# One ScalarE function table, scores of two heads from 64-row products, and a weight decode without Abs, in a fused attention and softplus expert kernel

## The chip, the cores and the metric

The kernel runs on one core of one Trainium2 chip. The core has a matrix engine (TensorE, PE in the profile, with its weight loads as PEld), a vector engine (VectorE, DVE), an engine for functions of one element (ScalarE, ACT), a general engine (GpSimd, POOL) and a queue engine (SyncE, SP) that issues transfers. The metric is the time of one execution on the device in microseconds, the median of the runs.

## The reference, cut to what matters

Attention over 4 batches, 8 heads, 576 tokens and 64 dimensions with a causal mask, mixed with a linear memory term by a gate per head, and then a two-layer expert with softplus between the layers (2304 tokens, 512 to 2048 to 512). Inputs q, k, v, M_prev, z_prev, beta are float32; the two expert weights come as float64.

```python
scores = scale * (q @ k^T)                    # scale = 1/8, causal mask
a = exp(scores - rowmax(scores))
a /= a.sum(-1) + 1e-9
local = a @ v
phi(x) = where(x > 0, x, exp(x) - 1) + 1
mem_out = (phi(q) @ M_prev) / (phi(q) @ z_prev + 1e-6)
g = 1 / (1 + exp(-beta))
x = g * mem_out + (1 - g) * local             # tokens x 512
h = x @ w_in
y = (max(h, 0) + log1p(exp(-abs(h)))) @ w_out # softplus between the layers
```

## The kernel before, in words

**Attention.** The work is cut into 16 units, one for each batch and pair of heads; a unit has five chunks of queries (four of 128 rows and one of 64). `emit_S` (lines 296 to 324) makes one chunk: scores of both heads into a PSUM tile `s`, a causal mask added by a product with an identity, the negated row maximum `nm` on VectorE, and the exponential on ScalarE straight from PSUM (line 318, or 322 for the last chunk), which also sums the row into `l`. The queries that feed the scores are copies `qs`, scaled by 1/8, in which the other head's 64 rows are zero, so that each head's product takes all 128 rows (line 301 with `qs`; `q1`, lines 239 to 243, makes the copies on ScalarE). `emit_split` (326 to 364) turns the exponentials into float16 high and low parts: high on GpSimd (line 342), low on VectorE (line 344), then a transposing transfer on the SP queue. `emit_pv` (line 385) multiplies by the values, 64 columns of the array for each head, the heads taking turns. The preparation of the next unit (`prep_items`: `v0` scale of the values, `f1` and `f2` phi(q), `f3` the memory product, `v1` and `v2` the float16 values) is spread over the chunks of the present one.

**Expert.** `emit_h` (line 144) makes one block of h: 12 products (`mm3`, line 134) of 288 tokens, with float32 numbers carried as two float32r parts. `emit_g` applies softplus to it as max(h,0) + log1p(exp(-|h|)) in eight instructions on ScalarE, GpSimd and VectorE (lines 159 to 166 and the helper at line 83), and splits the result into two parts (lines 89 and 83). A second group of 12 products takes it to the output accumulators `acc`. There are 16 blocks of d_ff in three groups of 5, 5 and 6. For the first group, four of the eight token blocks (20 calls of `emit_g`) are woven into the attention as filler, against a credit that grows with each chunk; the other 108 calls come after it. The weights arrive as the bits of float64 and are decoded by `split64` (lines 114 to 128): 32 pieces of 128x512, 10 during the attention, 22 after it while the products of the group before run.

**Order.** Each engine runs its own queue in order. A scheduler that works with modelled durations and with the priorities given in the code fixes the order of each queue when the program is built. Every ScalarE function comes from one table, loaded once at line 423.

## Time and profile before

| | before |
|---|---|
| time, median of 3 runs | 722.13 us (721.14 to 722.64) |
| span of the profiled execution | 718.0 us |
| PE / PEld busy | 636.2 us (89%) / 560.7 us (78%) |
| DVE busy | 585.8 us (82%) |
| ACT busy | 480.1 us (67%) |
| POOL busy | 389.4 us (54%) |
| chain that ended last, by engine | PE 40%, DVE 38%, ACT 7%, issue 6%, DMA 5%, POOL 4% |

The span runs from the first to the last instruction; the profile gives no other time for that execution, and the 4.1 us between the span and the median lie around it. The engines overlap, so that their busy times add up to far more than the span. PE's busy time holds the latency of its products too: a PE that is 100% busy in a stretch need not be at its fastest. The chain follows the work back from the last instruction, at each step to what released it.

### The profile page before, as it was taken

Reading aid. Unit: us, or ns where it says so; the run is one execution under the profiler, and the core shown is the slowest. Engines: PE = TensorE matmul, PEld = TensorE weight load, DVE = VectorE, ACT = ScalarE, POOL = GpSimd, SP = SyncE. Lnnn points to the kernel's source line nnn. Section 1 sums busy time; section 2 is a strip of 40 time slices with the busy share of each in tenths; the row PEclk is TensorE's granted clock in tenths of the full one; section 3 lists DMA queues with packets and bytes.
Section 4 is the critical chain, followed back from the end, with each engine's and each line's share of the span. In section 5 each row is a group of like instructions: output and inputs, shape, how many; then the busy total and the mean of one; then the engine's idle time right before and its main releaser. Section 6 shows DMA issues by size and latency. Waiting matters only on the chain.

```text
span 718.0 us, 13325 instructions
## 1 busy us (share of the span) xinstructions
PE 636.2 (89%) x4488; PEld 560.7 (78%) x4488; DVE 585.8 (82%) x1271; ACT 480.1 (67%) x1314; POOL 389.4 (54%) x495
## 2 busy tenths in 40 slices
PE   6587768979899889989788897888999999999997
PEld 5455546757777657768777896778999999999997
DVE  5899999996988998995899989998777655655644
ACT  7576677767767866864777685666666666666653
POOL 3456647774865864762466665565444334344342
PEclk9698978799999999999999999999999999999999
DMA  4988787576688678637522211210000000000101
GB/s 146 170 175 192 175 175 166 122 120 142 116 149 177 125 126 195 113 53 170 195 89 89 89 59 63 85 60 1 1 1 1 1 34 34 34 17 35 34 20 64
DMA packets 124179, 68.51 MB, mean 95 GB/s; under 512 B 105680, under 2 KB 113872, under 8 KB 124112
## 3 DMA queue, kind: packets, MB, share of 16 engines
q1 hardware_dynamic: 124112, 67.67, 40.9%
q8 instruction: 35, 0.57, 0.3%
q14 instruction: 32, 0.26, 0.1%
HBM read 34.89 MB, written 7.08 MB: 58 GB/s over the span
## 4 chain that ended last, share of the span: by engine, by line
PE 40%; DVE 38%; ACT 7%; issue 6%; DMA 5%; POOL 4%; SPq 0%; POOLq 0%; ACTq 0%; DVEq 0%
PE acc L134 16%; PE hp L134 16%; DVE PHL L344 6%; DVE l L166 4%; DVE c L165 3%; PE s L301 3%; DVE xhl L83 3%; DVE nm L316 3%; DVE wu L123 3%; DVE g L83 2%; DVE wu L125 2%; POOL PHL L342 2%; DVE wu L120 2%; ACT P L318 2%; DMA mq<-in_nat_dram 2%
## 5 line engine op out<-in xcount | busy, mean ns | idle before, releaser
L134 PE MATMUL hp<-xhl,w 128*128 128x288 f32 x1536 | 237.5, 303 | 8.6 <-ACT r L161 7.4
L134 PEld LDWEIGHTS hp<-xhl,w 128*128 128x128 f32 x1536 | 216.5, 193 | 12.3 <-ACT r L161 8.6
L134 PE MATMUL acc<-g,w 128*128 128x288 f32 x1296 | 190.0, 297 | 19.1 <-DVE g L83 9.4
L134 PEld LDWEIGHTS acc<-g,w 128*128 128x128 f32 x1296 | 176.7, 188 | 24.0 <-DVE g L83 11.8
L83 POOL TENSOR_TENSOR l<-l,c 128x288 f32<-128x288 f32 x128 | 116.0, 907 | 117.0 <-DVE l L166 109.2
L342 POOL TENSOR_SCALAR PHL<-P,rr 128x128 f16<-128x128 f32 (+3 forms) x128 | 85.4, 680 | 70.0 <-DVE rr L338 15.0
L163 POOL TENSOR_SCALAR c<-e 128x288 f32<-128x288 f32 x128 | 66.2, 518 | 85.1 <-ACT e L162 83.3
L301 PE MATMUL s<-kp,qs 128*128 128x128 f32 (+3 forms) x256 | 93.5, 494 | 9.8 <-ACT P L318 8.4
L344 DVE SCALAR_TENSOR_TENSOR PHL<-P,rr,PHL 128x128 f16<-128x128 f32 (+3 forms) x128 | 93.8, 751 | 7.3 <-POOL PHL L342 7.0
L165 DVE SCALAR_TENSOR_TENSOR c<-c,e 128x288 f32<-128x288 f32 x128 | 66.0, 516 | 37.4 <-ACT l L164 36.5
L318 ACT ACTIVATE P<-s,nm 128x128 f32<-128x128 f32 (+3 forms) x128 | 66.3, 525 | 41.6 <-DVE nm L316 36.6
L159 ACT ACTIVATE e<-hp 128x288 f32<-128x288 f32 x128 | 52.6, 411 | 57.1 <-PE hp L134 38.0
L164 ACT ACTIVATE l<-c 128x288 f32<-128x288 f32 x128 | 56.9, 445 | 45.8 <-DVE g L83 29.2
L83 DVE TENSOR_TENSOR g<-l,g 128x288 fp32r<-128x288 f32 x108 | 65.0, 603 | 26.5 <-ACT g L89 25.5
L89 ACT CAST g<-l 128x288 fp32r<-128x288 f32 x128 | 55.2, 432 | 28.0 <-POOL l L83 27.2
L166 DVE TENSOR_TENSOR l<-r,l 128x288 f32<-128x288 f32 x128 | 70.1, 548 | 0.0
L301 PEld LDWEIGHTS s<-kp,qs 128*128 128x128 f32 x256 | 46.7, 215 | 28.3 <-ACT P L318 10.6
L162 ACT ACTIVATE e<-e 128x288 f32<-128x288 f32 x128 | 57.3, 449 | 0.0
L83 POOL TENSOR_TENSOR w<-wu,w 128x512 fp32r<-128x512 f32 x32 | 49.1, 1535 | 14.2 <-ACT w L89 14.1
L385 PEld LDWEIGHTS <-vb 128*64 128x64 f16 x640 | 35.1, 116 | 26.4 <-issue 12.3
L316 DVE TENSOR_REDUCE nm<-s 128x2 f32<-128x256 f32 (+1 forms) x64 | 51.7, 810 | 4.7 <-PE s L304 4.6
L161 ACT ACTIVATE r<-hp 128x288 f32<-128x288 f32 x128 | 52.5, 410 | 3.5 <-DVE l L166 3.5
(85 smaller groups left out, 914.6 us busy)
## 6 DMA issues: line engine op xcount, KB each, us to landing
ws<-in_w_in_dram SPq DMA_DIRECT2D x16, 512.0 KB, 3.4
ws<-in_w_out_dram SPq DMA_DIRECT2D x16, 512.0 KB, 3.4
mq<-in_nat_dram SPq DMA_DIRECT2D x16, 353.0 KB, 3.4
va<-in_nat_dram SPq DMA_DIRECT2D x16, 320.0 KB, 3.2
kp<-in_nat_dram SPq DMA_DIRECT2D x16, 288.0 KB, 3.6
out_dram<-ps SPq DMA_DIRECT2D x32, 144.0 KB, 1.8
part<-pb SPq DMA_DIRECT2D x16, 144.0 KB, 2.4
ps<-part SPq DMA_DIRECT2D x4, 576.0 KB, 8.8
```

The lines of the kernel that those rows point to most:

```text
L83: eng.tensor_tensor(out=out, in0=in0, in1=in1, op=ALU.subtract)
L134: nc.tensor.matmul(out, lhsT=l, rhs=r, start=start and i == 0, stop=stop and i == n - 1)
L162: A.activation(out=e, in_=e, func=AF.Exp, scale=-1.0)
L163: P.tensor_scalar(out=c, in0=e, scalar1=1.0, scalar2=1.0, op0=ALU.mult, op1=ALU.add)
L164: A.activation(out=l, in_=c, func=AF.Ln)
L165: V.scalar_tensor_tensor(out=c, in0=c, scalar=-1.0, in1=e, op0=ALU.add, op1=ALU.subtract)
L166: V.tensor_tensor(out=l, in0=h, in1=l, op=ALU.add)
L301: nc.tensor.matmul(s[:, h, :n], lhsT=u.qs[:, 512 * h + c * 128:512 * h + (c + 1) * 128], rhs=u.kp[:, :n], start=True, stop=True)
L316: V.tensor_reduce(out=nm, in_=s[:, :, :n], op=ALU.max, axis=AX.X, negate=True)
L318: A.activation(out=pt[:, h * n:h * n + n], in_=s[:, h, :n], func=AF.Exp, bias=nm[:, h:h + 1], accum_out=l[:, h:h + 1])
L342: P.tensor_scalar(out=o[:, :, 0, h, :], in0=src, scalar1=r[:, h:h + 1], scalar2=0.0, op0=ALU.mult, op1=ALU.add)
L344: V.scalar_tensor_tensor(out=o[:, :, 1, h, :], in0=src, scalar=r[:, h:h + 1], in1=o[:, :, 0, h, :], op0=ALU.mult, op1=ALU.subtract)
```

## The change

Softplus replaces Exp and Ln as the one function of the ScalarE table. In `emit_g` one Softplus from PSUM takes the place of seven instructions. In the attention exp(y) is taken as softplus(y - 20), which is exp(y)·e^-20 to within float32 for y at or below 0; the factor e^-20 cancels through the row sums, the gates and the small constants. The scale 1/8 moves into the exponential's own scale, so the row maximum is multiplied by 1/8 and shifted by -20 in an added ScalarE instruction on a 128x2 tile (line 307 of the changed code), between the maximum and the exponential. The copies `qs` go, and each head's scores are a product over its own 64 rows of the query tile; the last chunk takes four products of 64 rows and 64 columns where it took two of 128 and 128. In `split64` the magnitude comes from a shift of the integer bits on VectorE, then a minimum and maximum on GpSimd, where it was ScalarE's Abs and a maximum on VectorE. In `v0` the mean magnitude comes from two Relu passes (of the value and its negative) and two small products, where it was one Abs pass and one product. The gates of beta are computed with Softplus as well.

```diff
 def split64(s, tu, hi, lo):
-        A.activation(out=tu, in_=sw[:, :, 1], func=AF.Abs)
-        V.tensor_scalar(out=tu, in0=tu, scalar1=TINY, scalar2=None, op0=ALU.max)
+        V.tensor_scalar(out=ti, in0=si[:, :, 1], scalar1=1, scalar2=1, op0=ALU.logical_shift_left,
+                        op1=ALU.logical_shift_right)
+        P.tensor_scalar(out=tu, in0=tu, scalar1=3.0e38, scalar2=TINY, op0=ALU.min, op1=ALU.max)
         V.tensor_scalar(out=ti, in0=ti, scalar1=3, scalar2=0x3FFFFFFF, op0=ALU.logical_shift_left,
                         op1=ALU.bitwise_and)
...
 def emit_g(pool, hp, n, cap, gb):
-        e = pool.tile([128, cap], F32, tag="e", name="e", bufs=2)
-        c = pool.tile([128, cap], F32, tag="c", name="c", bufs=2)
-        l = pool.tile([128, cap], F32, tag="l", name="l", bufs=2)
+        l = pool.tile([128, cap], F32, tag="l", name="l", bufs=3)[:, :n]
         g = pool.tile([128, 2, cap], F32R, tag="g", name="g", bufs=gb)
-        e, c, l = e[:, :n], c[:, :n], l[:, :n]
-        A.activation(out=e, in_=hp[:, :n], func=AF.Abs)
-        h = pool.tile([128, cap], F32, tag="r", name="r", bufs=2)[:, :n]
-        A.activation(out=h, in_=hp[:, :n], func=AF.Relu)
-        A.activation(out=e, in_=e, func=AF.Exp, scale=-1.0)
-        P.tensor_scalar(out=c, in0=e, scalar1=1.0, scalar2=1.0, op0=ALU.mult, op1=ALU.add)
-        A.activation(out=l, in_=c, func=AF.Ln)
-        V.scalar_tensor_tensor(out=c, in0=c, scalar=-1.0, in1=e, op0=ALU.add, op1=ALU.subtract)
-        V.tensor_tensor(out=l, in0=h, in1=l, op=ALU.add)
-        sub(P, l, l, c)
+        A.activation(out=l, in_=hp[:, :n], func=AF.Softplus)
         cast(A, g[:, 0, :n], l)
         sub(V if hcnt else P, g[:, 1, :n], l, g[:, 0, :n])
...
 def prep_items(i):
-        def q1():
-            for h in range(2):
-                r = slice(64 * h, 64 * h + 64)
-                A.mul(u.qs[r, 512 * h:512 * h + 512], u.qp[r, 0:512], 0.125)
-                A.mul(u.qs[r, 1024 + 64 * h:1088 + 64 * h], u.qp[r, 512:576], 0.125)
...
-            A.activation(out=jk, in_=u.vst, func=AF.Abs, accum_out=u.sc[:, 3:4])
+            for j, sg in enumerate((1.0, -1.0)):
+                A.activation(out=jk, in_=u.vst, func=AF.Relu, scale=sg, accum_out=u.sc[:, 3 + j:4 + j])
             sp = ps_r.tile([128, 512], F32, tag="sm", name="sp", bufs=1)
-            nc.tensor.matmul(sp[:, 0:1], lhsT=mean, rhs=u.sc[:, 3:4], start=True, stop=True)
+            for j in range(2):
+                nc.tensor.matmul(sp[:, 0:1], lhsT=mean, rhs=u.sc[:, 3 + j:4 + j], start=j == 0, stop=j == 1)
...
-            A.activation(out=u.pe, in_=u.pe, func=AF.Exp, scale=-1.0)
+            A.activation(out=u.pe, in_=u.pe, func=AF.Softplus, scale=-1.0, bias=msh)
...
 def emit_S(u, c):
             for h in range(2):
-                nc.tensor.matmul(s[:, h, :n], lhsT=u.qs[:, 512 * h + c * 128:512 * h + (c + 1) * 128],
-                                 rhs=u.kp[:, :n], start=True, stop=True)
+                r = slice(64 * h, 64 * h + 64)
+                nc.tensor.matmul(s[:, h, :n], lhsT=u.qp[r, c * 128:(c + 1) * 128], rhs=u.kp[r, :n],
+                                 start=True, stop=True)
...
             for i in range(2):
-                nc.tensor.matmul(s[:, i, :288], lhsT=u.qs[:, 1024:1152], rhs=u.kp[:, 288 * i:288 * i + 288],
-                                 start=True, stop=True)
+                for h in range(2):
+                    r = slice(64 * h, 64 * h + 64)
+                    nc.tensor.matmul(s[r, i, :288], lhsT=u.qp[r, 512:576], rhs=u.kp[r, 288 * i:288 * i + 288],
+                                     start=True, stop=True)
...
             V.tensor_reduce(out=nm, in_=s[:, :, :n], op=ALU.max, axis=AX.X, negate=True)
+            A.activation(out=nm, in_=nm, func=AF.Copy, scale=SCALE, bias=-SH)
             for h in range(2):
-                A.activation(out=pt[:, h * n:h * n + n], in_=s[:, h, :n], func=AF.Exp,
-                             bias=nm[:, h:h + 1], accum_out=l[:, h:h + 1])
+                A.activation(out=pt[:, h * n:h * n + n], in_=s[:, h, :n], func=AF.Softplus,
+                             scale=SCALE, bias=nm[:, h:h + 1], accum_out=l[:, h:h + 1])
...
-        A.preload_act_table_set("natural_log_exp_and_others")
+        A.preload_act_table_set("softplus")
```

Left out of the diff: the constants (SH = 20, ESH = e^-20, the tile `msh` that holds -20), the same edit of the exponential in the last chunk, the factor ESH at the small constants of `f2`, `f3` and `emit_split`, and the gates of beta in `consts`.

## Rows read from the trace of the kernel before

**Rows 1.** Busy time of each engine in five stretches. Columns: stretch, its length, busy us (instructions) of PE, PEld, DVE, ACT and POOL, the granted TensorE clock as a share of full speed, the DMA engines' busy share, GB/s.
```profile
0.00:160.00 160.00, 122.82 (x745) 88.20 (x746) 143.67 (x354) 109.37 (x294) 97.24 (x118) 0.85 0.75 161
160.00:328.00 168.00, 154.10 (x1118) 120.70 (x1117) 151.24 (x363) 118.84 (x340) 107.59 (x139) 0.98 0.69 135
328.00:345.00 17.00, 16.27 (x132) 15.09 (x131) 8.58 (x20) 8.95 (x24) 2.55 (x4) 1.00 0.73 193
345.00:500.00 155.00, 128.71 (x887) 122.85 (x886) 148.08 (x244) 107.79 (x286) 94.27 (x101) 0.97 0.23 77
500.00:718.00 218.00, 214.28 (x1615) 213.82 (x1613) 134.26 (x295) 135.11 (x373) 87.77 (x134) 1.00 0.07 23
```

**Rows 2.** The same view in short stretches: one of the attention, one of the last stage.
```profile
259.00:262.50 3.50, 3.50 (x9) 1.39 (x9) 3.22 (x9) 3.07 (x9) 2.83 (x5) 0.64 0.97 152
...
520.00:540.00 20.00, 20.00 (x153) 20.00 (x152) 14.97 (x31) 13.93 (x40) 8.71 (x13) 1.00 0.00 1
```

**Rows 3.** The waits of the stretch 328 to 500 us that hold PE. Columns: engine, its instruction and line, what it waited for, total us, times, longest us.
```profile
PEld acc L134 <- DVE g L83: 11.8, 10, 2.2
PEld hp L134 <- ACT r L161: 8.6, 5, 4.0
PEld acc L134 <- DVE ps L572: 8.0, 7, 1.8
```

**Rows 4.** Instructions of `emit_g`, grouped by line and shape. Columns: line, engine, operation, tiles written and read, shapes, count, busy us in total and mean ns of one, idle time of the engine before them with what ended it.
```profile
L159 ACT ACTIVATE e<-hp 128x288 f32<-128x288 f32 x128 | 52.6, 411 | 57.1 <-PE hp L134 38.0 <-DVE c L165 16.0 <-PE acc L134 2.3
L161 ACT ACTIVATE r<-hp 128x288 f32<-128x288 f32 x128 | 52.5, 410 | 3.5 <-DVE l L166 3.5
L162 ACT ACTIVATE e<-e 128x288 f32<-128x288 f32 x128 | 57.3, 449 | 0.0
L163 POOL TENSOR_SCALAR c<-e 128x288 f32<-128x288 f32 x128 | 66.2, 518 | 85.1 <-ACT e L162 83.3
L164 ACT ACTIVATE l<-c 128x288 f32<-128x288 f32 x128 | 56.9, 445 | 45.8 <-DVE g L83 29.2 <-POOL c L163 16.0
L165 DVE SCALAR_TENSOR_TENSOR c<-c,e 128x288 f32<-128x288 f32 x128 | 66.0, 516 | 37.4 <-ACT l L164 36.5
L166 DVE TENSOR_TENSOR l<-r,l 128x288 f32<-128x288 f32 x128 | 70.1, 548 | 0.0
L83 POOL TENSOR_TENSOR l<-l,c 128x288 f32<-128x288 f32 x128 | 116.0, 907 | 117.0 <-DVE l L166 109.2 <-DVE sc L255 3.9 <-DVE a L278 1.9
L83 DVE TENSOR_TENSOR g<-l,g 128x288 fp32r<-128x288 f32 x108 | 65.0, 603 | 26.5 <-ACT g L89 25.5
```

**Rows 5.** Instructions of `split64`, and the nearest GpSimd instruction of 512 elements with one tensor input; same columns.
```profile
L119 ACT ACTIVATE wu<-ws 128x512 f32<-128x512 f32 x32 | 21.6, 674 | 7.8 <-DMA ws<-in_w_out_dram 4.0 <-DMA ws<-in_w_in_dram 3.1 <-POOL w L83 0.8
L120 DVE TENSOR_SCALAR wu<-wu 128x512 f32<-128x512 f32 x32 | 19.3, 603 | 2.3 <-ACT wu L119 2.0
L121 DVE TENSOR_SCALAR wu<-wu 128x512 int32<-128x512 int32 x32 | 21.1, 659 | 0.3
L123 DVE SCALAR_TENSOR_TENSOR wu<-ws,wu 128x512 int32<-128x512 int32 x32 | 25.7, 803 | 0.2
L342 POOL TENSOR_SCALAR PHL<-P,rr 128x512 f16<-128x512 f32 x32 | 26.6, 843 | 18.1 <-issue 5.2 <-DVE rr L338 4.2 <-DVE a L280 2.8
```

**Rows 6.** The timeline from 348 us, in order of time. Columns: start us, length us, engine, line, operation, tiles, shapes, count, idle before.
```profile
348.57 3.13 POOL L83 TENSOR_TENSOR w<-wu,w 128x512 fp32r<-128x512 f32 x2
...
349.06 1.51 DVE L165 SCALAR_TENSOR_TENSOR c<-c,e 128x288 f32<-128x288 f32 x1
...
351.93 0.45 DVE L165 SCALAR_TENSOR_TENSOR c<-c,e 128x288 f32<-128x288 f32 x1
```

**Rows 7.** ScalarE instructions of the attention's preparation, and the smallest ScalarE instruction of the kernel, with the columns of rows 4.
```profile
L242 ACT ACTIVATE qs<-mq 64x512 f32<-64x512 f32 x32 | 20.0, 626 | 10.1 <-DMA mq<-in_nat_dram 9.8
L250 ACT ACTIVATE vb<-va 128x640 bf16<-128x640 f32 x16 | 11.7, 734 | 1.1 <-PE xp L385 1.0
L410 ACT ACTIVATE bsb<-bsb 128x8 f32<-128x8 f32 x1 | 0.2, 208 | 1.8 <-DMA bsb<-in_beta_dram 1.8
```

**Rows 8.** The longest wait for the row maximum in the stretch 165 to 328 us, with the columns of rows 3.
```profile
ACT P L318 <- DVE nm L316: 20.8, 12, 4.3
```

**Rows 9.** PE's timeline at three score chunks at the full clock (of 128, 512 and 288 columns; four matmul records each, two heads by two passes), at one of 512 columns in the stretch whose clock rows 2 give, and at one group of `emit_pv`; columns of rows 6.
```profile
268.09 0.61 PE L301 MATMUL s<-kp,qs 128*128 128x128 f32 x4
...
219.55 1.94 PE L301 MATMUL s<-kp,qs 128*128 128x512 f32 x4
...
264.17 1.24 PE L308 MATMUL s<-kp,qs 128*128 128x288 f32 x4
...
259.38 3.26 PE L301 MATMUL s<-kp,qs 128*128 128x512 f32 x4
...
222.53 1.72 PE L385 MATMUL xp<-PTB,vb 128*64 128x320 f16 x28
```

**Rows 10.** The forms of the records in that group of `emit_pv` (tile PTB), all units together; columns of rows 4.
```profile
L385 PE MATMUL xp<-PTB,vb 128*64 128x320 f16 x288 | 28.4, 313 | 6.0 <-DMA PTB<-PHL 6.0
L385 PE MATMUL xp<-PTB,vb 128*64 128x192 f16 x96 | 9.7, 252 | 0.0
L385 PE MATMUL xp<-PTB,vb 128*64 128x64 f16 x64 | 5.5, 197 | 0.0
```

**Rows 11.** The load of ScalarE's function table; columns of rows 4.
```profile
L423 ACT ACT_TABLE_LOAD x1 | 1.3, 1283 | 0.7 <-PEq L620 0.7
```

More of the change, by code (lines that the diff above doesn't have):

```diff
@@ L1 @@
+import math
 from collections import deque
@@ L24 @@
 TINY = 2.0 ** -15
+SH = 20.0
+SCALE = 0.125
+ESH = math.exp(-SH)
 GRPS = [5, 5, 6]
@@ L63, in attn_softplus_moe @@
     ident = res.tile([128, 128], F32, name="ident")
+    msh = res.tile([128, 1], F32, name="msh")
     g15 = res.tile([128, H], F32, name="g15")
@@ L219, in attn_softplus_moe @@
     at = attn_ctx.enter_context(tc.tile_pool(name="attn", bufs=1, side="right"))
-    qs_t = [at.tile([128, 1152], F32, name=f"qs{i}") for i in range(2)]
     def loads(i):
         u = units[i]
-        u.qs = qs_t[i % 2]
         b, p = u.b, u.p
@@ L237, in prep_items @@
         p = u.p
-        def q1():
-            for h in range(2):
-                r = slice(64 * h, 64 * h + 64)
-                A.mul(u.qs[r, 512 * h:512 * h + 512], u.qp[r, 0:512], 0.125)
-                A.mul(u.qs[r, 1024 + 64 * h:1088 + 64 * h], u.qp[r, 512:576], 0.125)
         def v0():
-            u.sc = at.tile([128, 4], F32, tag="sc", name="sc", bufs=3)
+            u.sc = at.tile([128, 5], F32, tag="sc", name="sc", bufs=3)
             si = u.sc.bitcast(I32)
@@ L262, in f1 @@
             A.activation(out=u.pe, in_=u.qp, func=AF.Relu, scale=-1.0)
-            A.activation(out=u.pe, in_=u.pe, func=AF.Exp, scale=-1.0)
+            A.activation(out=u.pe, in_=u.pe, func=AF.Softplus, scale=-1.0, bias=msh)
         def f2():
             u.ph = at.tile([128, S], F32, tag="ph", name="ph", bufs=1)
-            A.activation(out=u.ph, in_=u.qp, func=AF.Relu)
+            A.activation(out=u.ph, in_=u.qp, func=AF.Relu, scale=ESH)
             P.tensor_tensor(out=u.ph, in0=u.ph, in1=u.pe, op=ALU.add)
@@ L277, in f3 @@
                 nc.tensor.matmul(t[:, c - c0, :], lhsT=u.ph[:, q0:q0 + 128], rhs=u.mz, start=True, stop=True)
-            V.tensor_scalar(out=a, in0=t[:, :, 128:130], scalar1=1e-6, scalar2=None, op0=ALU.add)
+            V.tensor_scalar(out=a, in0=t[:, :, 128:130], scalar1=1e-6 * ESH, scalar2=None, op0=ALU.add)
             V.reciprocal(out=a, in_=a)
@@ L336, in emit_split @@
             nk = c + 1
-            V.scalar_tensor_tensor(out=r, in0=l, scalar=1e-9, in1=cinv[:, 2 * p:2 * p + 2], op0=ALU.add, op1=ALU.mult)
+            V.scalar_tensor_tensor(out=r, in0=l, scalar=1e-9 * ESH, in1=cinv[:, 2 * p:2 * p + 2], op0=ALU.add, op1=ALU.mult)
             V.reciprocal(out=r, in_=r)
@@ L349, in emit_split @@
             r = r[:, 0:1]
-            V.scalar_tensor_tensor(out=r, in0=l[:, 0:1], scalar=1e-9, in1=cinv4[:, p:p + 1], op0=ALU.add, op1=ALU.mult)
+            V.scalar_tensor_tensor(out=r, in0=l[:, 0:1], scalar=1e-9 * ESH, in1=cinv4[:, p:p + 1], op0=ALU.add, op1=ALU.mult)
             V.reciprocal(out=r, in_=r)
@@ L407, in consts @@
         P.memset(mean, 2.0 ** -7)
-        for t in qs_t:
-            P.memset(t, 0.0)
-        A.activation(out=bsb, in_=bsb, func=AF.Exp, scale=-1.0)
-        V.tensor_scalar(out=bsb, in0=bsb, scalar1=1.0, scalar2=None, op0=ALU.add)
-        V.reciprocal(out=bsb, in_=bsb)
-        V.tensor_scalar(out=cinv, in0=bsb, scalar1=-1.0, scalar2=1.0, op0=ALU.mult, op1=ALU.add)
-        V.tensor_scalar(out=cinv, in0=cinv, scalar1=PSC, scalar2=1e-30, op0=ALU.mult, op1=ALU.max)
+        P.memset(msh, -SH)
+        A.activation(out=cinv, in_=bsb, func=AF.Softplus)
+        A.activation(out=bsb, in_=bsb, func=AF.Softplus, scale=-1.0)
+        A.activation(out=bsb, in_=bsb, func=AF.Softplus, scale=-1.0, bias=msh)
+        A.activation(out=cinv, in_=cinv, func=AF.Softplus, scale=-1.0, bias=msh)
+        V.tensor_scalar(out=cinv, in0=cinv, scalar1=PSC / ESH, scalar2=1e-30, op0=ALU.mult, op1=ALU.max)
         V.reciprocal(out=cinv, in_=cinv)
```

9 lines of the change are left out of this document (5 added, 4 removed).

## The prediction

> **What bounds the kernel now.** I read the busy time by stretches first, because a share over the whole span mixes stages with different limits [rows 1]. Up to 328 us the kernel is in the attention: VectorE is busy 143.7 of the first 160 us (90%) and 151.2 of the next 168 (90%), with PE at 77% and 92%, ScalarE near 70%. From 328 to 345 us PE is full. From 345 to 500 us VectorE is busy 148.1 of 155 us (96%) while PE, at a granted clock of 0.97, is busy 128.7. From 500 us PE is never idle until the tail and VectorE has 62%.
>
> How far PE is from its pace in the third stretch is seen by counting. In the last stage 153 products take 20 us, 130.7 ns each [rows 2]. The 887 products of 345 to 500 us would take 887 x 0.1307 = 115.9 us at that pace; 39.1 us are lost there. The waits of that stage tell to whom: PE's weight loads wait for VectorE's low part of g (11.8 us), for ScalarE's Relu that frees the h tile (8.6), and for VectorE's accumulation (8.0) [rows 3]. So VectorE bounds two stages, PE the rest.
>
> **The change, part by part.**
>
> *emit_g.* Four ScalarE instructions (411, 410, 449, 445 ns) become one that reads the same PSUM tile; the table is not in the trace, so I bound it by the cheapest and dearest of these, 410 to 449, and take 411, that of the one with the same operands: 1.30 us less. VectorE loses 516 + 548 = 1.06 us, GpSimd 518 + 907 = 1.43 us [rows 4]. What remains, cast and subtraction, is unchanged. For 20 calls in the attention that is 21.3 us of VectorE; in 345 to 500 us, with 887/24 = 37 calls, 39.3 us; the rest lie where PE is full, and give nothing.
>
> *split64.* ScalarE loses 0.67 us for each piece. VectorE swaps a maximum (0.60) for a shift whose input has a stride of two; between the row of the same operation (0.66) and the one that reads the strided tile with a second input (0.80) I take 0.66, so +0.06, at most +0.20, and below nothing only as far as less GpSimd work lies beside it. GpSimd gains an instruction of one input; its row is 0.84 [rows 5]. VectorE's next instruction waits for it, and queued behind on VectorE are low parts of g and PE's accumulation. If the scheduler finds other VectorE work to put between, this costs nothing; if never, 22 x 0.84 = 18.5 us in the expert stage. I take 7, a third, and call this an estimate: the like wait today, for Abs, ends in 2.0 us in all [rows 5], but ScalarE's queue is freer than GpSimd's.
>
> *Attention, ScalarE.* The 512-column part of `q1` goes, 20.0 us; the second pass in `v0` adds 16 x 0.73 = 11.7; 80 instructions on `nm` add 80 x 0.21 = 16.6 by the smallest row [rows 7]; emit_g gives back 20 x 1.30 = 26.1, the ten decodes 6.7. Net 24 us less of 228 [rows 1], on an engine that is no bound. The instruction on `nm` matters by its place: it stands between maximum and exponential, where ScalarE already waits 20.8 us in the second stretch [rows 8], and it holds the score tile 0.2 us longer. With VectorE at 90% other units' work covers it; where the start has no cover, some 15 chunks at 0.2, it costs 3 us, and 80 x 0.21 = 17 us if it is covered nowhere.
>
> *Scores.* A chunk is four matmul records, two passes for each head: 0.61 us at 128 columns, 1.94 at 512 [rows 9]; between these lie 256 and 384 at some 1.05 and 1.50, so 5.1 us a unit, and 1.24 for the last chunk. Two products on different halves of the array can run beside each other: `emit_pv` shows it for columns. Its 28 records in 1.72 us [rows 9] are 18 of 320, 6 of 192 and 4 of 64 columns [rows 10], 7168 columns; at 130.7 ns for 288 [rows 2] they would take 3.25 us one by one. But there the heads alternate. Here each head brings two passes in a row, so that in order only the second of one head meets the first of the other: three slots of four, -1.3 us; the last chunk has eight records where it had four and fits them in five, +0.3. Net -1.0 a unit, 16 us of PE in the attention. The ends: all pairs meet, -2.55 x 16 = -41; none does, and the last chunk doubles, +20. The second small product in `v0` is two records of one column, less than half of the 0.61 us of four records of 128, so under 5 us of PE in all, inside these ends.
>
> *Loads.* The query tile is now read until the unit's last scores, as the key tile is already, so the load into its buffer starts later; on the SP queue the keys, the values and the transposing transfers stand behind it, but the keys waited for the same scores before. ScalarE waits 9.8 us for this load today, at `q1` [rows 7]; `f1` takes its place, and may wait as long again. 0 to +10 us; I take 0, since ScalarE has slack and VectorE needs what comes of it only a chunk later.
>
> The Trainium skill (TensorEngine Tiling (Array Packing), Key Properties) says against this that a change of tiling mode drains TensorE; each chunk would change it twice, around the mask product. No row isolates a drain; by that rule the 16 us would be less, and since VectorE sets the pace of both stretches the sum would hardly move.
>
> *The sum by stages, on the span of 718.0.* First 160 us: 5 of the 20 calls, 5.3 us of VectorE, less the 3 us of `nm`: -3 (bounds +3, when none of half the 80 links is covered, and -12, when the start without `qs` and less GpSimd traffic also count). 160 to 328: 15 calls, 16.0 us of VectorE; PE, busy 154.1 of 168, must follow, and may with half of the 16 us from the scores: 146. I take -15 (bounds: 0, if the stretches where PE is full only grow or `f1` waits; -30 if all pairs meet). 328 to 345: nothing. 345 to 500: VectorE's work falls to 148.1 - 39.3 + 1 = 110, under PE's 115.9, so PE becomes the bound; 39.1 less the 7 for the decode: -32 (bounds -20 and -39). Last stage: nothing, PE is the bound and its products are untouched. In all -50: a span of 668, and with the 4.1 us between span and median of the runs **672 us**.
>
> **Rivals.**
>
> *A. The attention gives nothing* (0 in both stretches, or the two cancel): the added link on `nm` and the decode's detour keep VectorE idle where it now works. For it: 80 added links, 20.8 us of waits at that place already. Against: 21 us of VectorE work leave a stage that is 90% VectorE. Time 722 - 32 = 690.
>
> *B. GpSimd's new instruction holds VectorE.* Today a VectorE instruction with two inputs takes 1.51 us while GpSimd subtracts and 0.45 beside an idle GpSimd [rows 6]. If each of the 22 new instructions stops VectorE for its own 0.84 us and the waits on it are exposed as well, the expert stage keeps 18.5 us of its loss: -20 there, 722 - 38 = 684. Against: GpSimd loses 37 x 1.43 = 53 us in that stage and gains 18.5, so VectorE should be held less, not more. The Trainium skill (GPSIMD Engine Reference, Specifications) has GpSimd sharing its SBUF interface with VectorE's instructions of two SBUF inputs; by that rule, the trace agrees.
>
> *C. More than forecast:* score pairs meet fully, and both stretches of the attention reach their lower bounds: -42 there, -32 to -39 later: 641 to 648. Against: VectorE's other 274 us of both stretches stay.
>
> *D. Slower: the clock.* The change takes work from PE in the attention, where its clock is already granted at only 0.85 on the mean over the first stretch with PE 77% busy [rows 1]. If PE has more pauses and the clock of the second stretch drops to the lower of its levels (1.2 GHz), its work lengthens: the four records of 512 columns took 3.26 us at a clock of 0.64 and 1.94 at full [rows 2, 9], a factor of 1.68, so 154 us become 259: +91 in that stretch against -35 elsewhere, some 778. It decides from about 47% of that stretch on (91 against the 15 not gained there, and 35). Against: the filler products keep that stretch at 0.98, and they run closer together afterwards.
>
> *E. The change doesn't do what it says:* if one of the functions used is not in the new table, it is loaded again and again, at 1.28 us each [rows 11]; 39 reloads undo the whole gain, and every emit_g would bring two. Against: only Softplus, Relu and Copy remain, and one table served four functions so far.
>
> **How the numbers follow.** Forecast (660 to 682): 0.50. A (683 to 698): 0.18; B (680 to 690): 0.12; C (640 to 659): 0.12; D: 0.04; E: 0.02; 0.02 for an attention that eats up what the expert stage gains. The range 650 to 697 holds the forecast, A, B and half of C, 0.86, less a few hundredths for the queue order, which the scheduler makes anew. A measurement of this kernel can tell 0.2% from no change. Faster by more than that: 0.93 (forecast, A, B, C and half of the last case); within it 0.02; slower 0.05 (nearly all of D and E).
>
> **What would show it.** In the profile of after: an expert stage where PE is never idle from some 310 us on, with 153 products in each 20 us while decodes still run; VectorE under 85% busy there; VectorE's busy time lower by 128 x 1.06 = 136 us and GpSimd's by 182 - 27 = 155. The last score accumulation ends near 310 us, not 328. Score chunks of 512 columns take some 1.5 us (three slots), not 1.94 nor 1.0. One load of the table. I am wrong if the expert stage still shows VectorE at 95% (then the decode's detour counts), if the attention ends at 325 us or later (A), or if the granted clock of the second stretch is under 0.9 (D).

## The result, and the profile after

The changed kernel takes **696.96 us** (median of 4 runs, 696.07 to 698.73) where the kernel before took 721.63 beside it: a ratio of 0.9676, interval 0.9649 to 0.9703. The forecast was 672. The time lies at the very end of the stated range, and of the 50 us forecast 25 came. The profiled execution has a span of 695.3 us. One version below, e3, ran in two groups, six runs of ten at 713 to 720 us and four at 701 to 708, and its ratio is of the faster four.

Busy time of each engine by stretches, after, in the columns of rows 1 and with the same limits:

```profile
0.00:160.00 160.00, 126.63 (x749) 80.17 (x750) 128.94 (x313) 90.27 (x263) 82.94 (x111) 0.78 0.66 151
160.00:328.00 168.00, 157.91 (x1178) 112.96 (x1176) 130.00 (x332) 108.44 (x337) 79.24 (x107) 0.98 0.69 139
328.00:345.00 17.00, 11.85 (x80) 8.46 (x80) 12.12 (x33) 7.17 (x22) 4.01 (x9) 0.81 0.41 70
345.00:500.00 155.00, 150.94 (x1142) 148.63 (x1137) 111.62 (x198) 68.10 (x178) 52.79 (x45) 1.00 0.31 96
500.00:695.30 195.30, 191.77 (x1446) 191.30 (x1444) 58.70 (x139) 60.39 (x152) 0.00 (x0) 1.00 0.07 25
```

Two stretches tell the story. From 345 to 500 us PE now does 1142 products where it did 887 [rows 1], and VectorE is busy 72% of it, not 96%. That is the expert stage as forecast. From 160 to 328 us VectorE is relieved as well (130.0 us, not 151.2), but nothing is finished sooner: from 328 to 345, where before PE was full with the expert, the attention is still running, and no engine is busy more than 71% of the time.

The instructions that the forecast priced, after, with the columns of rows 4:

```profile
L163 ACT ACTIVATE l<-hp 128x288 f32<-128x288 f32 x128 | 52.2, 411 | 139.2 <-PE hp L141 137.1 <-DVE g L89 2.1
L89 DVE TENSOR_TENSOR g<-l,g 128x288 fp32r<-128x288 f32 x108 | 57.9, 539 | 116.0 <-ACT g L95 116.0
L125 DVE TENSOR_SCALAR wu<-ws 128x512 int32<-128x512 int32 x32 | 13.9, 433 | 10.5 <-DMA ws<-in_w_in_dram 6.2 <-DMA ws<-in_w_out_dram 4.2
L127 POOL TENSOR_SCALAR wu<-wu 128x512 f32<-128x512 f32 x32 | 26.1, 817 | 54.3 <-DVE wu L125 44.8 <-DVE mem L273 3.2 <-DVE sc L245 2.5
L128 DVE TENSOR_SCALAR wu<-wu 128x512 int32<-128x512 int32 x32 | 18.2, 568 | 2.3 <-POOL wu L127 2.3
L310 ACT ACTIVATE nm<-nm 128x2 f32<-128x2 f32 x64 | 12.8, 202 | 75.7 <-DVE nm L309 75.5
L417 ACT ACT_TABLE_LOAD x1 | 1.3, 1283 | 0.7 <-PEq L614 0.7
```

Softplus takes 411 ns, the value taken for it; the table is loaded once. The added instruction on `nm` stands at line 310 of the changed kernel, not 307. The decode's shift takes 433 ns where 0.66 us was taken, GpSimd's part 817 where 0.84 was. Before the instruction that needs GpSimd's result (line 128) VectorE is idle for 2.3 us in the whole kernel: it hardly ever waits for the detour directly.

The score products, after, and the mask product behind a chunk, before and after (columns of rows 6):

```profile
162.24 0.49 PE L292 MATMUL s<-kp,mq 64*128 64x128 f32 x4
164.82 0.70 PE L292 MATMUL s<-kp,mq 64*128 64x256 f32 x4
150.26 0.92 PE L292 MATMUL s<-kp,mq 64*128 64x384 f32 x4
154.51 1.13 PE L292 MATMUL s<-kp,mq 64*128 64x512 f32 x4
155.58 0.29 PE L295 MATMUL s<-mask,identb 128*128 128x128 bf16 x2
158.39 1.19 PE L301 MATMUL s<-kp,mq 64*64 64x288 f32 x8
```

```profile
221.32 0.28 PE L304 MATMUL s<-mask,identb 128*128 128x128 bf16 x2
```

512 columns take 1.13 us against 1.94 [rows 9]: the pairs meet fully, not three slots in four, and the last chunk's eight records take no longer than its four did (1.19, 1.24 in rows 9). The mask product ends 0.23 us after the last score product (155.87 against 155.64), before it was 0.11 (221.60 against 221.49), so about 0.1 us a chunk is given back.

**Where the attention's time went.** I count the expert's products (lines 134 and 141) between three marks: the 8th, 24th and 32nd write of a finished piece of the attention into `x` (before 102.9, 268.4 and 337.7 us; after 113.8, 280.6 and 352.9), and go on to the 579th product. The view is that of the windows, for these products alone: stretch, length, PE's busy us (products), granted clock, DMA share, GB/s. Before, then after:

```profile
0.00:102.90 102.90, 4.51 (x18) 0.87 0.78 174
102.90:268.40 165.50, 55.80 (x316) 0.92 0.70 138
268.40:337.70 69.30, 31.26 (x185) 1.00 0.65 124
337.70:345.90 8.20, 8.20 (x64) 1.00 0.91 305
```

```profile
0.00:113.80 113.80, 6.51 (x18) 0.74 0.69 163
113.80:280.60 166.80, 71.72 (x411) 0.96 0.67 135
280.60:352.90 72.30, 21.05 (x123) 0.91 0.60 117
352.90:356.80 3.90, 3.85 (x29) 1.00 0.79 272
```

With a product at 130.7 ns [rows 2] this is an account. Start: 10.9 us lost. Middle: 1.3 us longer with 95 products more, worth 12.4, so 11.1 won. End: 3.0 us longer with 62 products fewer, worth 8.1, so 11.1 lost. The 579th product ends at 356.8 us, not 345.9: 10.9 late, where 18 early was forecast. What follows it takes 695.3 - 356.8 = 338.5 us against 718.0 - 345.9 = 372.1: 33.6 us won, where 32 was forecast. So the whole miss lies in the attention, and the experiments ask for the start and the end of it.

### The profile page after: what moved, and what is told of

It is laid out like the page before. It is cut to its first block, busy times and chain, and to the rows that moved or that the text cites. A ratio compares the mean times of both kernels' runs of the same rounds, so it can differ in the third digit from the quotient of the medians.

```text
span 695.3 us, 12560 instructions
## 1 busy us (share of the span) xinstructions
PE 639.1 (92%) x4584; PEld 541.5 (78%) x4584; DVE 441.4 (63%) x1012; ACT 334.4 (48%) x949; POOL 219.0 (31%) x270
## 4 chain that ended last, share of the span: by engine, by line
PE 37%; DVE 9%; DMA 3%; ACT 2%; issue 1%; POOL 1%; SPq 0%; DVEq 0%; ACTq 0%; POOLq 0%
PE acc L141 18%; PE hp L141 18%; DMA ws<-in_w_out_dram 2%; DVE wu L132 2%; DVE xhl L89 1%; DVE wu L130 1%; DVE wu L128 1%; DVE g L89 1%; DVE wu L125 1%; DVE PHL L339 1%; ACT P L312 1%; DVE ps L566 0%; DMA ws<-in_w_in_dram 0%; DMA PTB<-PHL 0%; ACT xhl L95 0%
## 5 line engine op out<-in xcount | busy, mean ns | idle before, releaser
L163 ACT ACTIVATE l<-hp 128x288 f32<-128x288 f32 x128 | 52.2, 411 | 139.2 <-PE hp L141 137.1
L292 PE MATMUL s<-kp,mq 64*128 64x128 f32 (+3 forms) x256 | 67.8, 567 | 13.0 <-ACT P L312 11.3
L380 PE MATMUL xp<-PTB,vb 128*64 128x320 f16 (+2 forms) x448 | 43.5, 290 | 7.2 <-DMA PTB<-PHL 6.9
L566 DVE TENSOR_TENSOR ps<-acc,ps 128x288 f32<-128x288 f32 x64 | 27.4, 456 | 35.2 <-PE acc L141 35.2
L310 ACT ACTIVATE nm<-nm 128x2 f32<-128x2 f32 x64 | 12.8, 202 | 75.7 <-DVE nm L309 75.5
L89 DVE TENSOR_TENSOR xhl<-x,xhl 128x288 fp32r<-128x288 f32 x80 | 37.1, 515 | 17.4 <-ACT xhl L95 17.4
L95 ACT CAST w<-wu 128x512 fp32r<-128x512 f32 x32 | 19.9, 621 | 53.3 <-DVE wu L132 53.3
L292 PEld LDWEIGHTS s<-kp,mq 64*128 64x128 f32 x256 | 25.2, 221 | 23.6 <-ACT P L312 13.3
L127 POOL TENSOR_SCALAR wu<-wu 128x512 f32<-128x512 f32 x32 | 26.1, 817 | 54.3 <-DVE wu L125 44.8
L141 PE MATMUL op<-g,w 128*128 128x288 f32 x240 | 42.2, 311 | 0.0
```

What stands on the lines that cost most here:

```text
L89: eng.tensor_tensor(out=out, in0=in0, in1=in1, op=ALU.subtract)
L95: A.copy(out, in_)
L127: P.tensor_scalar(out=tu, in0=tu, scalar1=3.0e38, scalar2=TINY, op0=ALU.min, op1=ALU.max)
L141: nc.tensor.matmul(out, lhsT=l, rhs=r, start=start and i == 0, stop=stop and i == n - 1)
L163: A.activation(out=l, in_=hp[:, :n], func=AF.Softplus)
L292: nc.tensor.matmul(s[:, h, :n], lhsT=u.qp[r, c * 128:(c + 1) * 128], rhs=u.kp[r, :n], start=True, stop=True)
```

## The experiments

All ratios are to the kernel before, run on the same chip. The changed kernel ran with the first result only, so a version is best set against it by its ratio, 0.9676 [0.9649, 0.9703]; the times come from several chips, on which the median of before lay between 719.3 and 721.6 us. A "mark" is a write into `x`, mostly the 8th, or the 579th product; the marks of a version come from its one profiled run.

**1. The score products.** e1 puts 128-row products back into the changed kernel (the copies `qs`, unscaled), e2 keeps 64 rows but reads them from a copy, so that the query tile is free early, and e4 puts 64-row products, from a scaled copy, into the kernel before.

```diff
 # e1
-nc.tensor.matmul(s[:, h, :n], lhsT=u.qp[r, c * 128:(c + 1) * 128], rhs=u.kp[r, :n],
+nc.tensor.matmul(s[:, h, :n], lhsT=u.qs[:, 512 * h + c * 128:512 * h + (c + 1) * 128], rhs=u.kp[:, :n],
 # e2, and e4 in the kernel before (there qc = 0.125 * qp)
+A.mul(u.qc, u.qp, 1.0)
+nc.tensor.matmul(s[:, h, :n], lhsT=u.qc[r, c * 128:(c + 1) * 128], rhs=u.kp[r, :n],
```

> The kernel after, with the scores again from 128-row products of zero-padded copies of the query tile (unscaled, the scale stays in the exponential), and so with the copies on ScalarE and the query tile free early. Theory P (the 64-row products: each chunk changes the array's tiling twice, the mask products went from some 62 to 117 ns and the four-product last chunk from 1.1 to 1.5 us, and the clock of the first 140 us fell from 0.83 to 0.74): the last attention write comes at 335 us or earlier, not 352, the clock of the first 140 us is back over 0.8, time 678 to 686. Theory N (the added link on the row maximum costs the attention its gain): no change from 697. Theory L (the query tile held to the unit's last scores delays its loads and what stands behind them on the SP queue): also 680 to 688, but then the run with 64-row products from a copy gains as much.

Measured: 699.52 us, 0.9714 [0.9681, 0.9746]. The 8th write is back at 103.0 us, so the start's loss is gone, and the total is no better; the last write comes at 350.7, where theory P had 335. Start and middle of e1, in the view of the marks:

```profile
0.00:103.00 103.00, 4.82 (x18) 0.83 0.71 164
103.00:281.50 178.50, 69.84 (x402) 0.94 0.69 138
```

The middle takes 11.7 us more than in the changed kernel and holds 9 products fewer, some 13 us lost. PE is nearly full there, so the 64-row products may be worth a part of it; but e6, which has them in nearly all of this stretch, loses 7.7 us in it too (table in 6).

> The kernel after, with the 64-row products fed from a copy of the query tile (one ScalarE pass of 576 columns a unit), so that the tile that is loaded is free early, as before. Theory L (late loads): 682 to 690, waits of the SP queue's query loads for the scores gone (16.5 us in the kernel after). Theory P and theory N: 697 to 700, the copy costs what it costs.

Measured: 701.49 us, 0.9749 [0.9716, 0.9781], the 8th write at 120.1. The queue's waits of the query load for the scores are gone, and nothing is gained (the copy costs a ScalarE pass): late loads are not the cause.

> The kernel before, with its scores from 64-row products of one scaled copy of the query tile and nothing else changed: Exp and Ln, Abs, no link on the row maximum, query tile free early. Theory P: 730 to 738, the clock of the first 140 us lower than 0.83, the attention later by 10 to 15 us. Theories N and L: 714 to 722, since PE has less to do and ScalarE 12 us less.

Measured: 727.91 us, 1.0112 [1.0079, 1.0145]. In the kernel before the cheaper products cost 8 us: the 8th write comes at 107.4, the middle takes 170.5 us (165.5 before), and the last write is 10.8 us late, at a clock of 0.78 over the first 140 us (0.84 before). The time lies between the ranges of the two theories. Less PE work alone is no gain here; why it costs isn't shown.

**2. The link on `nm`.** e3 moves the added instruction to VectorE, e8 leaves it out (the exponential then takes the raw maximum; the values are not the reference's).

```diff
 # e3
-A.activation(out=nm, in_=nm, func=AF.Copy, scale=SCALE, bias=-SH)
+V.tensor_scalar(out=nm, in0=nm, scalar1=SCALE, scalar2=-SH, op0=ALU.mult, op1=ALU.add)
 # e8
-A.activation(out=nm, in_=nm, func=AF.Copy, scale=SCALE, bias=-SH)
```

> The kernel after, with the scaling and shift of the row maximum on VectorE right behind the maximum, instead of on ScalarE. Theory N (the link on ScalarE's queue): 685 to 692, since the hand-over to ScalarE's queue is done once. Theories P and L: 696 to 700, 80 x 0.15 us more on a VectorE that is busy 77% of the attention.

Measured: 0.9779 [0.9744, 0.9814], which is some 704 us beside the 720 of before; the best of its ten runs took 701.43, more than any of the changed kernel (696.07 to 698.73). No gain from the other engine.

> The kernel after, without the ScalarE instruction that scales and shifts the row maximum: the exponential takes the raw negated maximum as its bias, so its values are not those of the reference. Theory N (the link on the row maximum costs the attention several us): 685 to 691. Theories C and F: 694 to 697, since ScalarE is busy 64% of the attention and a wait of 0.2 us for each chunk is covered by another unit's work.

Measured: 692.81 us, 0.9605 [0.957, 0.964], the 8th write at 102.5. Without the link the start's 10.9 us are gone, yet only some 4 us are won in all, less than theory N asked: the middle takes 179.2 us for 340 products (after 166.8 for 411), and the end 68.9 for 194 (after 72.3 for 123).

**3. The decode.** e9 puts the new decode alone into the kernel before; e14 puts the minimum and maximum of the changed kernel on VectorE, so that GpSimd has no part in it.

```diff
 # e9, in the kernel before
-A.activation(out=tu, in_=sw[:, :, 1], func=AF.Abs)
-V.tensor_scalar(out=tu, in0=tu, scalar1=TINY, scalar2=None, op0=ALU.max)
+V.tensor_scalar(out=ti, in0=si[:, :, 1], scalar1=1, scalar2=1, op0=ALU.logical_shift_left,
+                op1=ALU.logical_shift_right)
+P.tensor_scalar(out=tu, in0=tu, scalar1=3.0e38, scalar2=TINY, op0=ALU.min, op1=ALU.max)
 # e14, in the changed kernel
-P.tensor_scalar(out=tu, in0=tu, scalar1=3.0e38, scalar2=TINY, op0=ALU.min, op1=ALU.max)
+V.tensor_scalar(out=tu, in0=tu, scalar1=3.0e38, scalar2=TINY, op0=ALU.min, op1=ALU.max)
```

> The kernel before, with the new weight decode alone (shift on VectorE, minimum and maximum on GpSimd, no Abs on ScalarE). If the decode has a share in the expert stage's gain, the expert stage (counted from the 579th product, 372 us in the kernel before) gets shorter by 3 us or more and the time is 714 to 718. If emit_g alone made that gain, as the sum of VectorE's work says (39 of 40 us), the time is 720 to 728: VectorE still bounds the stage, and now waits for GpSimd as well.

Measured: 738.52 us, 1.0254 [1.0216, 1.0292], far more than the waits on it show:

```profile
L121 POOL TENSOR_SCALAR wu<-wu 128x512 f32<-128x512 f32 x32 | 25.3, 791 | 11.8 <-DVE wu L119 6.8 <-DVE a L281 1.7 <-DVE sc L256 1.1
L122 DVE TENSOR_SCALAR wu<-wu 128x512 int32<-128x512 int32 x32 | 17.9, 561 | 0.0
```

VectorE is never idle before the instruction that needs GpSimd's result (0.0). By the marks, 12.4 us are lost up to the 579th product and 3.6 after it. The start is not slower, its 8th and 16th writes come at 99.2 and 179.2 us (before 102.9 and 191.6). But at the 16th 84 products are done, before it was 196; the filler has fallen behind, and the next eight writes take 97.7 us with 237 products (before 76.8 with 138). That another order of the queues does this is my reading; no run isolates it.

> The kernel after with the decode's minimum and maximum on VectorE, so that VectorE no longer waits for GpSimd between the shift and the mask. Theory D (the way through GpSimd costs the attention, as the 19 us of the kernel before with the new decode suggest): 688 to 693, with the attention's last write before 348 us. Theory F: 695 to 702, since the expert stage has a VectorE with room and the attention's end stays bare.

Measured: 691.24 us, 0.9613 [0.9574, 0.9653]. The 579th product comes 7.8 us sooner (349.0), what follows takes 3.1 longer (341.6), and the last write comes at 343.3, as theory D asked: in this version the detour's absence helps the attention and costs the expert stage.

**4. The clock.** From 0 to 160 us the granted clock is 0.78 after and 0.85 before [rows 1]. e7 adds four dummy products, whose result goes nowhere, to each of the first 20 chunks.

```diff
+if t < 20:
+    for _ in range(4):
+        nc.tensor.matmul(hp[:, :256], lhsT=ident, rhs=pt[:, :256], start=True, stop=True)
```

> The kernel after, with four float32 products of 256 columns added in each of the first 20 chunks, which read the chunk's exponentials and whose result is used nowhere. Theory C: the clock of the first 140 us goes above 0.85, the 8th attention write comes before 110 us, and the time falls by 3 to 8 us although PE has 20 x 1.7 us more to do. Theory O (the first stretch is set by the order of the queues and the hand-overs, not by the clock): 700 to 710.

Measured: 693.21 us, 0.9599 [0.9556, 0.9642]. The clock over the first 140 us rises from 0.74 to 0.87, yet the 8th write comes at 121.6, later still; and e8 reached it at 102.5 with 0.72. The clock doesn't explain the start. The time did fall as theory C said (0.9599 against 0.9676); the marks come from a run of 697.83 us, and the other three took 690.74 to 694.63, so where that gain lies stays open.

**5. The filler.** In the changed kernel no product of the expert is left to weave in when the attention nears its end. The same view as for the marks, in slices of 20 us; 516 products are done by the 28th write at 325.4 us:

```profile
280.00:300.00 20.00, 9.38 (x58) 1.00 0.82 171
300.00:320.00 20.00, 4.61 (x29) 0.91 0.49 99
320.00:340.00 20.00, 0.11 (x1) 0.88 0.56 98
340.00:360.00 20.00, 14.00 (x89) 0.87 0.65 160
```

Before, the slice 320 to 340 holds 92, and the last four of the 32 writes have 104 products beside them; after, 36. e5 raises the credit of the filler, which takes a fifth block of tokens into the attention; e11 does the same to the kernel before; e13 keeps four blocks, but the fourth is one that the attention finishes only with its third batch, so that it can't be done early.

```diff
 # e5, e11
-credit = min(credit + 0.8 * (1, 2, 3, 4, 2.25)[c] / 2.45, 3)
+credit = min(credit + 1.0 * (1, 2, 3, 4, 2.25)[c] / 2.45, 3)
 # e13
-if k < NFILL:
+if k < NFILL and k != 3:
```

> The kernel after, with the filler's credit rate at 1.0 where it was 0.8, so that five token blocks of the expert's first group are woven into the attention and not four. Theory F (the shorter softplus lets the scheduler run the filler earlier: at the 24th of the 32 attention writes 429 expert products are done where the kernel before had 334, and from the 28th on none is left, so that PE stands bare at the attention's end): the bare stretch of some 28 us takes up part of the 120 products of a fifth block, 15.7 us at PE's pace, and the time falls by 5 to 12 us, to 685 to 692. Theory Q (PE simply has no room in the attention): the attention ends 15 us later and the time stays at 695 to 700.

Measured: 687.20 us, 0.9521 [0.9476, 0.9566]: 9.8 us less than the changed kernel. Its middle, the first line, is that of the changed kernel with 21 products more; its end takes longer and holds 212 products, not 123:

```profile
114.20:278.10 163.90, 73.15 (x432) 0.97 0.65 137
278.10:359.70 81.60, 34.86 (x212) 0.90 0.55 110
```

At 130.7 ns a product the middle gains 5.6 us and the end only 1.9, and the slice from 320 to 340 us still holds no more than 21 products. The time is the one that theory F asked for, the place mostly isn't.

> The kernel before with the filler's credit rate at 1.0 alone. Theory F: the kernel before has no bare end (filler runs to its last units) and VectorE is full there, so a fifth block only lengthens the attention: 718 to 726. If instead more filler helps any version of this kernel, and the bare end is no effect of the change: 709 to 714.

Measured: 724.94 us, 1.0081 [1.0055, 1.0106]. The kernel before has nothing to gain from it: it has no such gap, the change opened it.

> The kernel after with the same amount of filler, four token blocks at the same credit, but the fourth is the first block of the third batch (block 4) and not the last of the second (block 3), so that its inputs exist only from the 24th attention write on. Theory F (the filler is used up early and PE stands bare at the end): fewer products done at the 24th write (under 400 where 429 were), products still being done after the 28th, and 686 to 692. If only the amount of filler counts: 694 to 700.

Measured: 691.64 us, 0.9596 [0.9557, 0.9636]. No more filler, only later: 5.3 us less than the changed kernel. 378 products are done at the 24th write and 463 at the 28th (after 429 and 516), and the gain lies in the end, 9.5 us there. The gap at the end is a cause.

**6. Put together.** e6 keeps 128-row scores in the first five units only, where the start is lost, and 64 rows after. e10 adds e5's credit, e12 a credit of 1.25, e15 e13's late block to e10. e17 is e10 with e14's decode, e18 e5 with it.

```diff
 # e6: qs as in e1, for the first five units
+u.qs = qs_t[i % 2] if i < 5 else None
...
+if u.qs is not None:
+    nc.tensor.matmul(s[:, h, :n], lhsT=u.qs[:, 512 * h + c * 128:512 * h + (c + 1) * 128],
+                     rhs=u.kp[:, :n], start=True, stop=True)
+    continue
```

> The kernel after, with 128-row score products from zero-padded copies in the first five units, where there is no filler, and 64-row products from then on. Theory C (the 64-row products halve PE's work where PE has little to do, the granted clock of the first 140 us falls from 0.84 to 0.74 and the 8th attention write comes at 114 us where it came at 103; later, where PE is full, they save PE's time): the 8th write at 103 us, the pace after it as in the kernel after, time 684 to 690. If the scheduler's order and not the clock makes the early difference: within 2 us of 697.

Measured: 690.06 us, 0.9567 [0.9528, 0.9607], the 8th write at 107.1, not 103. The pace after it isn't that of the changed kernel either: the middle loses 7.7 us and the end wins 6.5.

> The kernel after, with both edits that gained: 128-row score products in the first five units and the filler's credit rate at 1.0. If the two losses are separate (filler that runs out: 10 us; the slow first stretch: 7 us) the gains add up: 678 to 683. If they are one and the same loss, 685 to 690.

Measured: **682.85 us**, 0.9526 [0.9444, 0.9607], the lowest median of this study, with runs from 681.10 to 691.92. Its ratio is no lower than that of e5, 0.9521 [0.9476, 0.9566], so it isn't shown that the two gains add up. Its middle and end:

```profile
105.80:279.40 173.60, 73.12 (x413) 0.93 0.68 138
279.40:353.60 74.20, 38.42 (x242) 1.00 0.63 124
```

Read with the end of before (69.3 us with 185 products) and after (72.3 with 123): 242 products ride along in nearly the same time, and PE is busy 71.6 of the 74.2 us, in the changed kernel 60.4 of 72.3. The last quarter of the attention takes some 9 us a write in these three (10.2 in e5), and what isn't woven into it is paid for later.

> The kernel of the last run but one (128-row products in the first five units) with the credit rate at 1.25, which weaves six blocks. If PE still has bare stretches at the attention's end: 672 to 678. If five blocks fill them: 679 to 686, with the attention's end later by about what the sixth block takes, 15.7 us.

Measured: 691.01 us, 0.9569 [0.9505, 0.9633]. Still more credit gives nothing more (runs from 684.94 to 695.45).

> All that gained together: the kernel after with 128-row score products in the first five units, the credit rate at 1.0 and the blocks 0, 1, 2, 4, 5 as filler, so that two of five come from the third batch. Theory F: 674 to 681, under the 682.9 of the same kernel with blocks 0 to 4. If filler is plentiful there already: 681 to 686.

Measured: 689.86 us, 0.9587 [0.9563, 0.961]: a miss, the late block and the larger credit don't add up.

> 128-row scores in the first five units, filler credit 1.0 and the decode's minimum and maximum on VectorE, together. If the three causes are separate, the decode's share (5.7 us of the changed kernel's time when it was tried alone) comes on top of the version with the other two (682.9): 676 to 680. If the decode's detour only cost time because the filler ran out late in the attention, it is paid for already: 682 to 687, since VectorE does 32 more instructions of about 0.6 us, most of them in the expert stage, where the version without the detour lost some 3 us.

Measured: 695.2 us, 0.9614 [0.9554, 0.9674]: worse than either expectation. Its 8th write comes at 110.3, its 24th at 291.1 (279.4 in e10).

> As the run before, but with the 64-row scores in all units: filler credit 1.0 and minimum and maximum on VectorE. Separate causes: 687.2 less 5.7, 680 to 684. One cause seen twice: 686 to 690, the same as with the credit alone.

Measured: 687.56 us, 0.9542 [0.9492, 0.9591], the same as e5, as one cause seen twice would have it. So e14's gain doesn't add to the filler's. Each edit makes the scheduler order all queues anew; I take the scatter among these versions for that, but no run isolates it.

**The marks side by side.** Each stretch set against the changed kernel, in us, less or more products counted at 130.7 ns each; minus is a gain. Products count that had ended at a mark (the windows above also count those that cross it, hence 10.7 here for 11.1 there).

| profiled run | to the 8th write | 8th to 24th | 24th to 32nd | after it | span |
|---|---|---|---|---|---|
| before | -10.9 | +11.1 | -10.7 | +33.2 | +22.7 |
| e1, 128-row scores | -10.8 | +13.1 | -4.5 | +2.9 | +0.7 |
| e8, no link | -11.3 | +21.7 | -12.7 | -0.3 | -2.6 |
| e14, decode on VectorE | -9.4 | +1.2 | -1.4 | +4.9 | -4.7 |
| e6, 128 rows in five units | -6.7 | +7.7 | -6.5 | +0.7 | -4.8 |
| e10, e6 with more credit | -8.0 | +6.7 | -13.7 | -1.1 | -16.1 |
| e5, more credit | +0.4 | -5.6 | -1.9 | -1.6 | -8.8 |
| e13, later block | +1.6 | +1.6 | -9.5 | 0.0 | -6.3 |

A start that is won back doesn't stay won: in e1, e6, e8 and e10 the middle takes most or all of it again, and their 16th write comes at 196.5 to 201.4 us, that of the changed kernel at 199.4. Only e14 keeps it (192.0). The filler counts in the end: in e13, and in e10 by 7.2 us against e6, which differs by the credit alone.

**What a bad order looks like.** The changed kernel near 107 us, one chunk of 512 columns and what VectorE does meanwhile (columns of rows 6):

```profile
99.81 1.13 PE L292 MATMUL s<-kp,mq 64*128 64x512 f32 x4
...
100.87 0.28 PE L295 MATMUL s<-mask,identb 128*128 128x128 bf16 x2
...
102.82 1.46 DVE L339 SCALAR_TENSOR_TENSOR PHL<-P,rr,PHL 128x256 f16<-128x256 f32 x1
...
104.47 0.57 DVE L270 SCALAR_TENSOR_TENSOR a<-a,sc,g 128x6 f32<-128x6 f32 x1
105.08 0.56 DVE L273 TENSOR_TENSOR mem<-np,a 128x384 f32<-128x384 f32 x1
...
106.38 0.43 DVE L125 TENSOR_SCALAR wu<-ws 128x512 int32<-128x512 int32 x1 [0.21 <-DMA ws<-in_w_out_dram]
...
106.72 0.61 DVE L339 SCALAR_TENSOR_TENSOR PHL<-P,rr,PHL 128x384 f16<-128x384 f32 x1
...
107.25 1.22 DVE L309 TENSOR_REDUCE nm<-s 128x2 f32<-128x1024 f32 x1
...
108.50 0.20 ACT L310 ACTIVATE nm<-nm 128x2 f32<-128x2 f32 x1 [5.85 <-DVE nm L309]
...
110.29 0.79 PE L292 MATMUL s<-kp,mq 64*128 64x128 f32 x2 [2.71 <-ACT P L312]
```

The scores are complete at 101.15, the maximum starts at 107.25: it stands in VectorE's queue behind the low parts and the memory product of other chunks and the shift of a decode. ScalarE waits 5.85 us at the link, the score tile stays taken, and PE waits 2.71 for it. Over the first 160 us such waits grew:

```profile
ACT nm L310 <- DVE nm L309: 35.0, 15, 5.9
```

```profile
ACT P L318 <- DVE nm L316: 15.8, 11, 3.5
```

```profile
ACT P L311 <- DVE nm L309: 34.2, 18, 6.3
```

The first is after, the second before, the third e8, all from 0 to 160 us. VectorE was busy 81% of that stretch after, so I put these waits down to its order and not its load. But e8 has them as well, and its 8th write comes at 102.5 us: they show what a chunk loses, not what the 10.9 us of the start are made of.

## Why the prediction was right and wrong

**Right: the expert stage.** "PE becomes the bound" there, -32: it is -33.6 by the 579th product. VectorE lost 585.8 - 441.4 = 144.4 us in all (136 forecast), GpSimd 389.4 - 219.0 = 170.4 (155). From 360 to 380 us PE does 154 products while decodes still run:

```profile
360.00:380.00 20.00, 20.00 (x154) 20.00 (x153) 16.92 (x30) 11.29 (x30) 8.66 (x8) 1.00 0.55 176
```

In the four slices from 380 to 460 us it does 150, 140, 143 and 146, some 4.3 us short of that pace. The 7 us for the decode's detour is not seen as such: VectorE waits 2.3 us for it in all, e14 has the stage 3.1 us longer without the detour and e9, in the kernel before, 3.6 longer with it. What it costs stays open.

**Wrong: the attention, -3 and -15.** The step that failed is "VectorE bounds two stages": a busy share of 90% was read as the limit of the attention, and 21 us of VectorE work less as time. Its busy time did fall, by 36 us (143.7 to 128.9 and 151.2 to 130.0), and the time did not follow: the last score product starts at 336.4 us (before 319.3) and the last write comes at 352.9 (before 337.7), past the 325 us that the prediction named as a sign of being wrong. What sets the pace instead is not isolated. My reading is the round of one chunk through PE, VectorE, ScalarE, GpSimd and the transfers, in the order in which the queues hold them: in the last part it takes some 9 us a write with 123 products beside it or with 242 (e10), and in the changed kernel VectorE is busy 67% of that part. In the middle PE is a rival, busy 157.7 of 166.8 us; no run tells the two apart.

The second failed step is one that the prediction left out: it counted the filler's gain only as VectorE time, and not how many products the attention carries. 95 more of them ran in the middle, 11 us won of the 15 in the sum, but they were taken from the end, where nothing was left to fill (e13, and e10 against e6, with e11 as the control). That the shorter softplus chain lets the scheduler bring them forward is argued, not shown, and e8 speaks against the chain as the only reason: it has the same chain and 358 products at the 24th write, not 429.

The third is the start: "3 us" for the link on `nm` and -3 in all, measured +10.9 at the 8th write. Taking back the score products (e1), the link (e8) or the detour (e14, 104.4) each gives nearly all of it back, alone. Three causes of 9 to 11 us can't add up to 10.9, so these are no separate prices, and the same decode makes the start of the kernel before 3.7 us faster (e9). That the order of the queues decides is my reading; which instruction out of place costs the start stays open, and e1 and e8 have lost most or all of the gain again by the 16th write.

**The score products** were mis-sized the other way. "Three slots of four" (1.5 us for 512 columns) is two slots, 1.13 us. A unit's five chunks take 0.49 + 0.70 + 0.92 + 1.13 + 1.19 = 4.43 us, not 0.61 + 1.05 + 1.50 + 1.94 + 1.24 = 6.34 [rows 9, the two in the middle as the prediction put them], less about 0.1 for each mask product: some -1.5 a unit, not -1.0. The Trainium skill (TensorEngine Tiling (Array Packing), Key Properties) has a change of tiling mode drain the array; the mask product's 0.23 us instead of 0.11 is what this trace shows at that place, and it is no bar to the pairs.

**The rivals.** A was nearest: 690 if the attention gives nothing; it gave less than nothing. B's mechanism, GpSimd holding VectorE, is seen, but small:

```profile
450.63 0.44 DVE L89 TENSOR_TENSOR g<-l,g 128x288 fp32r<-128x288 f32 x1
...
451.50 0.99 POOL L127 TENSOR_SCALAR wu<-wu 128x512 f32<-128x512 f32 x1 [2.41 <-DVE wu L125]
...
451.93 0.86 DVE L89 TENSOR_TENSOR g<-l,g 128x288 fp32r<-128x288 f32 x1
```

Beside the decode's GpSimd instruction alone, 32 VectorE instructions of the expert stage take 3.0 us more in all than their like beside an idle GpSimd, where B had 18.5; in the attention it is 0.3. C's first half came (pairs meet fully), its second didn't. D's condition didn't come: the clock from 160 to 328 us is 0.98; only that of the first stretch fell, 0.85 to 0.78. E fell with the single table load.

## What to carry to other kernels

An engine that is 90% busy in a pipelined stage need not be its bound: here 36 us less work on it moved no write forward. Time the round of one chunk, see whether any stretch of it runs bare, and set more than one mark, since what is won at one can be lost by the next. Work that fills gaps has to last until the end of what it fills; when a change makes it shorter, give it more or make it later, and run the same edit on the old kernel as a control. An edit that shows no wait (the decode, 0.0) cost 18 us all the same, by a new order of the queues as I read it, so try each part of a change alone.

## What was not expected of the hardware

Float32 products of 64 rows on different halves of the array ran in pairs, although the program issues one head's product behind the other's: eight records of 288 columns in 1.19 us, four of 128 rows in 1.24 before. In the chunk of 512 columns at 154.51 us the records of a pair start 6 ns apart, and the next pair 0.53 us after the first; records of 128 rows and 512 columns followed each other every 0.43 us. So a pair takes a quarter longer than a single record, not twice as long. GpSimd's instruction with one tensor input also held VectorE's subtraction with two: 0.86 us beside it, 0.44 without (rivals, B). The granted clock and the progress of the start went apart: the 8th write at 102.5 us with a mean clock of 0.72 over the first 140 us (e8), at 121.6 with 0.87 (e7).
